# Single PSUM banks in turn for the expert passes, the passes' last part in common code, and a weight slot loaded from ScalarE's queue

## The chip, the cores and the metric

One Trainium2 chip, one core of it. The metric is the device time of one execution in microseconds (us); less is better. TensorE (PE) does the matrix products, VectorE (DVE) and ScalarE (ACT) read its results out of PSUM (eight banks of 2 KB per partition), GpSimd (POOL) issues the indexed transfers, SyncE (SP) most of the others.

## The reference

A banded attention, and behind it a layer of eight experts of which every token takes one. `x` has 3072 tokens of 512 numbers, an expert has 512 x 1024 and 1024 x 512 weights, all in float32:

```python
a = softmax(scale * q @ k.T + bias, over a band of 96 and the first 8 keys)
x = (a @ v) as (3072, 512)
expert_idx = argmax(x @ w_gate, axis=1)
probs = softmax(x @ w_gate)
gate_w = probs[n, expert_idx]
for e in range(8):
    mask = expert_idx == e
    h = maximum(x[mask] @ w1[e], 0)
    out[mask] = gate_w[mask] * (h @ w2[e])
```

## The kernel before

Attention takes the first 208 us of the span. Then comes the routing: tokens are scattered, sorted by expert, into a buffer in memory (`xs_dram`), and gathered from there. The experts run from about 246 us to 644 us, and a tail of 21 us ends the kernel.

**What an expert is made of.** The first 128 tokens of an expert e are its small part: `x_in_s(e)` (line 775) transposes them on PE into a PSUM tile and DVE copies them to `xsT` (line 776); `up_s(e)` (lines 786 and 790) multiplies by w1 and applies Relu on ACT; `down_s(e)` (lines 796 and 798) multiplies by w2, DVE multiplies by the gate into `ys`, and POOL scatters `ys` to the output. The rest of the tokens is its pass, n tokens wide. n is known only at run time, so the pass is written in 10 forms (n = 0, or 128 to 384 in steps of 32), and a switch at run time branches to one of them. With this input the passes e = 0 to 7 take the forms 352, 288, 256, 288, 256, 288, 288 and 160.

**What a form does**, in the order of PE's program, which is written by hand:
- up: for each of 8 slices f of the hidden layer, 4 matmuls into `ph` (line 893), then Relu on ACT into `hT` (line 895).
- `x_in(e+1, 0)` and `x_in(e+1, 1)` (line 858): 8 transposes of the next expert's tokens, which DVE copies to `xT` (line 859).
- down: for each of 4 slices d of the output, 8 matmuls into `py` (line 900), then an ACT copy into `yT` (line 902). From d = 1 on, `back(d-1)` stands behind each: it transposes `yT` on PE into a `pt` tile (line 881), and DVE multiplies by the gate into `y` (line 883 for the whole blocks of 128 tokens, line 887 for the rest).
- `x_in(e+1, 2)` behind `back(0)`, `x_in_s(e+2)` (line 775) behind `back(1)`; at the end of the form `back(3)` and then the scatters of `y` (line 733, on POOL; one for each begun block of 128 tokens).

**Common code between two forms**: the weights of expert e+3 are asked for on SP's queue, POOL gathers for e+2 and e+4, PE does `up_s(e+2)` and `down_s(e+2)`, and the next switch follows. PE, ACT, DVE and POOL all take part in the switch; SP doesn't.

**PSUM.** The two `ph` tiles have two banks each and hold two slices f each; there are two `pt` tiles and two `py` tiles of one bank, taken by the number of the block, the slice or the expert (d % 2, t % 2, e % 2). A wait goes by the tile, so a slice that is written into the second bank of a `ph` tile waits for the Relu that still reads the first one. The pools are the ones that the attention uses.

The weights lie in three slots. Those of experts 0 and 1 are loaded during the attention; the third slot lies where the attention's tiles were, and is loaded behind it by `fetch(2)`, four transfers of 1 MB on SP's queue. A float32 matmul of the program is two records in the trace.

```python
ph = self.ph[f // 2 % 2][:, f % 2, 0:n]      # up, slice f
pt, g = self.t[d % 2], self.gate[e % 2]      # back(d)
x, pt = self.xg[e % 2], self.t[t % 2]        # x_in(e, t)
x, pt = self.xs[e % 2], self.t[e % 2]        # x_in_s(e)
```

Of the kernel before, what the change touches and what calls it, by code (L numbers as in the profile page):

```python
# [20 lines left out]
def kernel(  # L21
# [666 lines left out]
    class Experts:  # L688
        def __init__(self, stack, rt, psum):
            self.rt = rt  # L690
            ps_s, ps_t, ps_o, ps_r = self.psum = psum
# [80 lines left out]
        def x_in_s(self, e):  # L772
            x, pt = self.xs[e % 2], self.t[e % 2]
# [8 lines left out]
        def up_s(self, e):  # L782
            for f in range(NFC):
                ph = self.ph[f // 4 % 2][:, 0, :]
                for c in range(NDC):
                    nc.tensor.matmul(ph[:, ts(f % 4, P)], lhsT=self.w[e % 3][0][:, c, ts(f, P)],  # L786
                                     rhs=self.xsT[e % 2][:, c, :], start=(c == 0), stop=(c == NDC - 1),
                                     skip_group_check=True)
                if f % 4 == 3:
                    nc.scalar.activation(self.hsT[:, f - 3:f + 1, :].rearrange("p a b -> p (a b)"), ph,  # L790
                                         AF.Relu)

        def down_s(self, e):
            py = self.py[e % 2]
            for f in range(NFC):
                nc.tensor.matmul(py[:], lhsT=self.hsT[:, f, :], rhs=self.w[e % 3][1][:, f, :],  # L796
                                 start=(f == 0), stop=(f == NFC - 1))
            nc.vector.tensor_scalar(self.ys[:], py[:], self.gates[:, e:e + 1], None, ALU.mult)  # L798
            self.scatter(self.ys[:], self.tos[:, e:e + 1])


        def begin(self, stack):

            ps_s, ps_t, ps_o, ps_r = self.psum
# [50 lines left out]
        def x_in(self, e, t):  # L855
            x, pt = self.xg[e % 2], self.t[t % 2]
# [10 lines left out]
        def one_pass(self, e, n, between):  # L867

            w1t, w2t = self.w[e % 3]
            xT, hT, y = self.xT[e % 2], self.hT, self.y[e % 2]  # L870
# [6 lines left out]
            def back(d):  # L877
                pt, g = self.t[d % 2], self.gate[e % 2]
                for t in range(0, n, P):
                    m = min(P, n - t)  # L880
                    nc.tensor.transpose(pt[0:m, t // P, :], self.yT[d % 2][:, t:t + m], ident[:])  # L881
                full = n // P
                nc.vector.tensor_tensor(y[:, 0:full, ts(d, P)], pt[:, 0:full, :],  # L883
                                        g[:, 0:full].unsqueeze(2).to_broadcast([P, full, P]), ALU.mult)
                if n % P:
                    m = n % P
                    nc.vector.tensor_scalar(y[0:m, full, ts(d, P)], pt[0:m, full, :], g[0:m, full:full + 1],  # L887
                                            None, ALU.mult)

            for f in range(NFC if n else 0):  # L890
                ph = self.ph[f // 2 % 2][:, f % 2, 0:n]
# [5 lines left out]
            for d in range(NDC if n else 0):  # L897
                py = self.py[d % 2][:, 0:n]
# [4 lines left out]
                if d:  # L903
                    back(d - 1)
                if d in (1, 2):
# [20 lines left out]
        def passes(self, judge):  # L926
            for e in range(E):
                index = {eng: self.forms[e] for eng in self.ENGINES}
                for i in tc.Switch(index, len(WIDTHS), hint=f"pass{e}"):
                    more = []  # L930
# [15 lines left out]
                if e + 3 < E:  # L946
                    self.up_s(e + 2)
                    self.down_s(e + 2)
                elif e + 2 < E:
                    self.up_s(e + 2)  # L950
                    judge()
                elif e + 1 < E:
                    self.down_s(e + 1)
# [4 lines left out]
    with ExitStack() as stack, tc.manual_schedule(engines={PE}):  # L958
        psum = [stack.enter_context(tc.tile_pool(name=f"ps_{nm}", bufs=n, space=bass.MemoryType.PSUM))
                for nm, n in (("s", 2), ("t", 2), ("o", 1), ("r", 1))]  # L960
        pool, rows = router_pools(stack)
        ex = Experts(stack, rt, psum)
        with ExitStack() as inner:
# [75 lines left out]
```

## Time and profile before

| | us |
|---|---|
| runs: median of 3 (lowest, highest) | 671.41 (669.81, 676.6) |
| the profiled execution | 667.69 |
| its span | 665.5 |
| PE busy in the span | 563.6 (85%) |
| DVE, ACT, POOL busy | 176.4, 125.2, 104.4 |
| mean granted clock of PE, of full speed | 0.965 |

The profile is of one execution. The span runs from the first to the last instruction that it shows; 2.2 us lie around it. The times in the rows below count from the start of the span.

### The profile page before, as it was taken

What the parts mean: (1) busy time and instruction counts of PE and PEld (TensorE: products, weight loads), DVE (VectorE), ACT (ScalarE), POOL (GpSimd) and SP (SyncE); (2) the same over time, 40 slices, a digit from 0 to 9 for tenths busy, and PEclk for the clock granted to TensorE, in tenths of its full rate; (3) what the DMA queues carried; (4) which work ended last, traced back from release to release, by engine and by line L of the source; (5) the groups of instructions that cost most, each with busy time, mean ns of one, the idle gap of its engine ahead of it and who ended that gap; (6) DMA issues with size and microseconds to landing.
All of it is one profiled execution on the core that took longest, in us unless ns stands there. A gap on an engine that the chain in (4) does not pass through costs nothing.

```text
span 665.5 us, 11159 instructions
## 1 busy us (share of the span) xinstructions
PE 563.6 (85%) x4541; PEld 434.8 (65%) x4541; DVE 176.4 (27%) x520; ACT 125.2 (19%) x237; POOL 104.4 (16%) x148
## 2 busy tenths in 40 slices
PE   3699699698799968999988898898999998889860
PEld 2588578587588635576666686577678576766660
DVE  6756456566363210110020020011001002002010
ACT  1353343435232001100100110110111110110100
POOL 3000400400501550013004002101301200100110
PEclk9799899999999989999998999999999999899995
DMA  9999997557513740334117035133433200100100
GB/s 165 250 258 215 271 233 169 166 138 159 178 33 118 258 146 0 126 91 135 57 75 226 1 127 179 51 127 105 127 126 131 68 0 3 58 0 3 40 24 19
DMA packets 98312, 77.48 MB, mean 116 GB/s; under 512 B 79194, under 2 KB 79194, under 8 KB 98144
## 3 DMA queue, kind: packets, MB, share of 16 engines
q1 hardware_dynamic: 90240, 56.63, 30.8%
q0 software_dynamic: 6544, 18.98, 8.8%
q8 instruction: 56, 0.92, 0.6%
q14 instruction: 112, 0.92, 0.4%
q10 hardware_dynamic: 1360, 0.04, 0.1%
HBM read 60.92 MB, written 12.89 MB: 111 GB/s over the span
## 4 chain that ended last, share of the span: by engine, by line
PE 70%; DVE 9%; issue 8%; ACT 4%; DMA 3%; POOL 2%; another core or an unknown queue 1%; ACTq 0%; POOLq 0%; DVEq 0%
PE ph L893 19%; PE py L900 18%; PE ph L786 8%; PE py L796 6%; PE po L358 4%; PE sp L336 4%; DVE p L347 2%; PE pr L369 2%; ACT hT L895 2%; PE pt L225 2%; PE px L380 2%; DMA xs_dram<-xr,slot_i 2%; PE pt L858 2%; PE pt L881 1%
## 5 line engine op out<-in xcount | busy, mean ns | idle before, releaser
L893 PE MATMUL ph<-xT,w 128*128 128x288 f32 (+3 forms) x512 | 131.1, 408 | 20.1 <-ACT hT L895 19.3
L893 PEld LDWEIGHTS ph<-xT,w 128*128 128x128 f32 x512 | 93.6, 194 | 58.5 <-ACT hT L895 33.0
L900 PE MATMUL py<-hT,w 128*128 128x288 f32 (+3 forms) x512 | 121.3, 393 | 0.0
L900 PEld LDWEIGHTS py<-hT,w 128*128 128x128 f32 x512 | 92.3, 190 | 21.3
L733 POOL DMA_INDIRECT out_dram<-y,to x21 | 20.5, 974 | 321.1 <-DVE y L887 241.4
L786 PE MATMUL ph<-xsT,w 128*128 128x128 f32 x512 | 61.2, 281 | 9.1 <-issue 3.7
L786 PEld LDWEIGHTS ph<-xsT,w 128*128 128x128 f32 x512 | 59.6, 196 | 11.6 <-issue 10.6
L348 ACT ACTIVATE p<-p 128x1024 f32<-128x1024 f32 (+1 forms) x48 | 47.0, 983 | 85.3 <-DVE p L347 78.2
L895 ACT ACTIVATE hT<-ph 128x288 f32<-128x288 f32 (+3 forms) x64 | 25.4, 397 | 180.7 <-PE ph L893 177.7
L796 PE MATMUL py<-w,hsT 128*128 128x512 f32 x128 | 56.3, 593 | 0.6 <-issue 0.6
L347 DVE SCALAR_TENSOR_TENSOR p<-sp,other 128x1024 f32<-128x1024 f32 x40 | 47.4, 1216 | 13.4 <-remote 11.6
L336 PE MATMUL sp<-qt,kt 64*128 64x128 f32 x448 | 41.0, 294 | 11.0 <-DVE p L347 7.2
L859 DVE COPY xT<-pt 128x512 f32<-128x512 f32 x24 | 15.8, 687 | 118.0 <-PE pt L858 118.0
L883 DVE TENSOR_TENSOR y<-pt,gate 128x256 f32<-128x256 f32 (+1 forms) x32 | 13.1, 408 | 119.5 <-PE pt L881 118.9
L358 PE MATMUL po<-p,vt 128*64 128x128 f32 x448 | 39.9, 277 | 4.7 <-issue 4.7
L336 PEld LDWEIGHTS sp<-qt,kt 64*128 64x128 f32 x448 | 34.0, 205 | 12.4 <-issue 11.7
L796 PEld LDWEIGHTS py<-w,hsT 128*128 128x128 f32 x128 | 23.7, 190 | 27.6 <-issue 27.6
L902 ACT COPY yT<-py 128x288 f32<-128x288 f32 (+3 forms) x32 | 12.3, 385 | 130.7 <-PE py L900 130.7
L358 PEld LDWEIGHTS po<-p,vt 128*64 128x64 f32 x448 | 27.3, 138 | 7.5 <-issue 7.3
L798 DVE TENSOR_SCALAR ys<-py,gates 128x512 f32<-128x512 f32 x8 | 6.0, 751 | 95.4 <-PE py L796 40.2
L336 PE MATMUL sp<-qt,ka 64*128 64x128 f32 x256 | 27.2, 290 | 0.0
L726 POOL DMA_INDIRECT xg<-xs_dram,grow x24 | 24.6, 1024 | 14.4 <-issue 6.1
(151 smaller groups left out, 498.2 us busy)
## 6 DMA issues: line engine op xcount, KB each, us to landing
w<-in_moe_w_dram SPq DMA_DIRECT2D x32, 1024.0 KB, 7.0
raw_q<-in_q_dram SPq DMA_DIRECT2D x24, 256.0 KB, 4.0
raw_k<-in_k_dram SPq DMA_DIRECT2D x24, 256.0 KB, 4.5
vt<-in_v_dram SPq DMA_DIRECT2D x24, 256.0 KB, 4.2
va<-vt SPq DMA_DIRECT2D x16, 192.0 KB, 4.1
va<-vt SPq DMA_DIRECT2D x16, 64.0 KB, 4.0
xs_dram<-xr,slot_i POOLq DMA_INDIRECT x24
xg<-xs_dram,grow POOLq DMA_INDIRECT x24
```

The lines of the kernel that those rows point to most:

```text
L336: nc.tensor.matmul(sp[:, a, j, t, :], lhsT=kt[r, 2 * g + j, :], rhs=qts[n][r, 2 * g + j, :], start=True, stop=True, skip_group_check=True)
L347: nc.vector.scalar_tensor_tensor(z, sc, QS, bi, ALU.mult, ALU.add)
L348: nc.scalar.activation(z, z, AF.Exp)
L358: nc.tensor.matmul(po[D * a:D * a + D, m, :], lhsT=vt[:, 2 * m + a, :], rhs=ps[n][m // 2][:, a, m % 2, t, :], start=(x == 0), stop=(x == l ...
L726: nc.gpsimd.indirect_dma_start(out=dst.bitcast(I32), out_offset=None, in_=xs_dram[:], in_offset=bass.IndirectOffsetOnAxis(ap=idx, axis=0), ...
L733: d = nc.gpsimd.indirect_dma_start(out=out[:], out_offset=bass.IndirectOffsetOnAxis(ap=idx, axis=0), in_=src, in_offset=None, bounds_check ...
L786: nc.tensor.matmul(ph[:, ts(f % 4, P)], lhsT=self.w[e % 3][0][:, c, ts(f, P)], rhs=self.xsT[e % 2][:, c, :], start=(c == 0), stop=(c == ND ...
L796: nc.tensor.matmul(py[:], lhsT=self.hsT[:, f, :], rhs=self.w[e % 3][1][:, f, :], start=(f == 0), stop=(f == NFC - 1))
L859: nc.vector.tensor_copy(out=self.xT[e % 2][:, :, ts(t, P)], in_=pt[:])
L893: nc.tensor.matmul(ph, lhsT=w1t[:, c, ts(f, P)], rhs=xT[:, c, 0:n], start=(c == 0), stop=(c == NDC - 1), skip_group_check=True)
L895: nc.scalar.activation(hT[:, f, 0:n], ph, AF.Relu)
L900: nc.tensor.matmul(py, lhsT=w2t[:, f, ts(d, P)], rhs=hT[:, f, 0:n], start=(f == 0), stop=(f == NFC - 1), skip_group_check=True)
```

## The change

Five things change in the experts, none in the attention:
- **PSUM.** The experts get a pool of their own, with eight tiles of one bank: three named `ph`, two `py`, three `t`. Each user takes the next one in turn. Slice f of the up part then uses the bank of slice f-3. The attention's pools are released before the experts begin.
- **Order in a form.** `x_in(e+1, 2)` moves behind `back(1)` and `x_in_s(e+2)` behind `back(2)`, which is the end of the form.
- **The last part.** `back(3)` and the scatters of `y` leave the form. `finish(e)` does them in common code, always for 384 tokens (3 transposes, 1 DVE multiply, 3 scatters), behind the first half of `up_s`, or in the last two passes behind the first half of `down_s(7)` and alone. Since unused rows are then read too, `clear_y` sets `y` and `yT` to zero once, on POOL. POOL takes no part in the switch any more.
- **Halves.** `up_s` and `down_s` are written in two halves; the work is the same.
- **Weights of expert 2.** `fetch(2)` is issued on ACT's queue, and stands behind `up_s(1)` in the program.

The core of the diff:

```diff
-        def fetch(self, e):
+        def fetch(self, e, queue=nc.sync):
...
-                    nc.sync.dma_start(out=dst[:, a:a + n // 2, :], in_=s_[:, a:a + n // 2, :])
+                    queue.dma_start(out=dst[:, a:a + n // 2, :], in_=s_[:, a:a + n // 2, :])
...
-            self.ph = [ps_s.tile([P, 2, 512], F32, tag="s", name=f"ph{i}") for i in range(2)]
-            self.t = [ps_t.tile([P, 4, P], F32, tag="t", name=f"pt{i}") for i in range(2)]
-            self.py = [ps_o.tile([P, 512], F32, tag="o", name="py0"),
-                       ps_r.tile([P, 512], F32, tag="r", name="py1")]
+            ps = stack.enter_context(tc.tile_pool(name="ps_e", bufs=1, space=bass.MemoryType.PSUM))
+            self.bank = {nm: [ps.tile([P, 4, P], F32, name=f"{nm}{i}") for i in range(n)]
+                         for nm, n in (("ph", 3), ("py", 2), ("t", 3))}
+        def turn(self, nm):
+            self.used[nm] += 1
+            return self.bank[nm][self.used[nm] % len(self.bank[nm])]
+        def clear_y(self):
+            for i in range(2):
+                nc.gpsimd.memset(self.y[i][:], 0.0)
+                nc.gpsimd.memset(self.yT[i][:], 0.0)
...
-                ph = self.ph[f // 2 % 2][:, f % 2, 0:n]
+                ph = self.turn("ph")[:].rearrange("p a b -> p (a b)")[:, 0:n]
...
                 if d:
-                    back(d - 1)
-                if d in (1, 2):
+                    self.back(e, d - 1, n)
                     other()
...
-            if n:
-                back(NDC - 1)
-            for t in range(0, n, P):
-                m = min(P, n - t)
-                self.scatter(y[0:m, t // P, :], self.to[e % 2][0:m, t // P:t // P + 1])
-        ENGINES = (PE, mybir.EngineType.Activation, mybir.EngineType.DVE, mybir.EngineType.Pool)
+        def finish(self, e):
+            self.back(e, NDC - 1, TP * P)
+            for t in range(TP):
+                self.scatter(self.y[e % 2][:, t, :], self.to[e % 2][:, t:t + 1])
+        ENGINES = (PE, mybir.EngineType.Activation, mybir.EngineType.DVE)
...
                         more.append(lambda: (self.x_in(e + 1, 0), self.x_in(e + 1, 1)))
+                        more.append(lambda: None)
                         more.append(lambda: self.x_in(e + 1, 2))
...
-                if e + 3 < E:
-                    self.up_s(e + 2)
-                    self.down_s(e + 2)
...
+                for fn in parts[:1] + [lambda: self.finish(e)] + parts[1:]:
+                    fn()
```

**PE, the form of 288 tokens of pass 3 and the common code behind it.** `ph`, `pt` (in the changed kernel `t`) and `py` with a number are PSUM tiles, `xs` the gathered tokens of a small part, `w_0` and `w_2` weight slots. Before:

```order
L893 MATMUL ph_2921<-xT_2911,w_0_131 128x288 x8
L893 MATMUL ph_2922<-xT_2911,w_0_131 128x288 x8
...
L881 MATMUL pt_2924<-ident,yT_2914 128x128 x2
L881 MATMUL pt_2924<-ident,yT_2914 32x128
L775 MATMUL pt_2924<-ident,xs_145 128x128 x4
L900 MATMUL py_2926<-hT,w_0_132 128x288 x8
L881 MATMUL pt_2923<-ident,yT_2913 128x128 x2
L881 MATMUL pt_2923<-ident,yT_2913 32x128
L881 MATMUL pt_2924<-ident,yT_2914 128x128 x2
L881 MATMUL pt_2924<-ident,yT_2914 32x128
...
L786 MATMUL ph_2921<-xsT_147,w_2_2906 128x128 x16
L786 MATMUL ph_2922<-xsT_147,w_2_2906 128x128 x16
```

And in the changed kernel:

```order
L891 MATMUL ph_2930<-xT_2915,w_0_119 128x288 x4
L891 MATMUL ph_2928<-xT_2915,w_0_119 128x288 x4
L891 MATMUL ph_2929<-xT_2915,w_0_119 128x288 x4
...
L869 MATMUL t_2935<-ident,xg_2912 128x128 x4
L898 MATMUL py_2932<-hT,w_0_120 128x288 x8
L912 MATMUL t_2933<-ident,yT_2917 128x128 x2
L912 MATMUL t_2933<-ident,yT_2917 32x128
L774 MATMUL t_2934<-ident,xs_133 128x128 x4
...
L786 MATMUL ph_2929<-xsT_135,w_2_2910 128x128 x16
L912 MATMUL t_2935<-ident,yT_2918 128x128 x3
L786 MATMUL ph_2930<-xsT_135,w_2_2910 128x128 x16
```

Eight matmuls in a row went to one `ph` tile, and now four do, with three tiles in turn. The transposes of `xs`, which had a whole down slice behind them, are now the last work of the form, directly ahead of the `up_s` that reads their copy; the form's last `back` stands between the halves of `up_s`.

**POOL, the end of the program.** `TENSOR_LOAD bad_i` reads the flag on which the kernel ends or runs again. Before:

```order
L733 DMA out_dram<-y_2916,to_2918 3072x512 x2
L929 ISA
L1034 UNCONDITIONAL_BRANCH
...
L733 DMA out_dram<-y_2916,to_2918 3072x512 x3
L1034 UNCONDITIONAL_BRANCH
L733 DMA out_dram<-ys,tos 3072x512
L1000 TENSOR_LOAD bad_i
```

And in the changed kernel:

```order
L732 DMA out_dram<-y_2919,to_2921 3072x512 x3
L732 DMA out_dram<-ys,tos 3072x512
L1061 UNCONDITIONAL_BRANCH
L732 DMA out_dram<-y_2920,to_2922 3072x512 x3
L1027 TENSOR_LOAD bad_i
```

The rows of before are two of the last pass's forms, of which the switch takes one, and the common code behind them, with the last scatter of `ys` in it. In the changed program POOL has no forms: one path, in which the last three scatters of `y` stand behind that of `ys`, directly ahead of the flag.

## Rows read from the trace of the kernel before

**Rows 1.** Page, engines: busy us (share of the span), records
```profile
PE 563.6 (85%) x4541; PEld 434.8 (65%) x4541; DVE 176.4 (27%) x520; ACT 125.2 (19%) x237; POOL 104.4 (16%) x148
```

**Rows 2.** PE's waits, 245 to 665 us: total us, times, longest
```profile
PE ph L893 <- ACT hT L895: 19.3, 32, 2.1
PE pt L858 <- DVE y L887: 3.8, 5, 0.8
PE ph L786 <- issue: 3.7, 2, 2.3
...
PE pt L775 <- DVE y L887: 2.3, 3, 0.8
```

**Rows 3.** Timeline, PE, pass 3: start, us, records, idle before
```profile
419.46 2.10 PE L893 MATMUL ph<-xT,w 128*128 128x288 f32 x8
...
426.90 4.15 PE L893 MATMUL ph<-xT,w 128*128 128x288 f32 x16 [0.56 <-ACT hT L895]
...
438.36 1.04 PE L858 MATMUL pt<-ident,xg 128*128 128x128 f32 x8
439.23 7.93 PE L900 MATMUL py<-hT,w 128*128 128x288 f32 x32
447.00 0.49 PE L881 MATMUL pt<-ident,yT 128*128 128x128 f32 x3
...
448.75 4.05 PE L900 MATMUL py<-hT,w 128*128 128x288 f32 x16
452.63 0.49 PE L881 MATMUL pt<-ident,yT 128*128 128x128 f32 x3
...
454.38 4.05 PE L900 MATMUL py<-hT,w 128*128 128x288 f32 x16
458.26 0.49 PE L881 MATMUL pt<-ident,yT 128*128 128x128 f32 x3
...
460.32 7.38 PE L786 MATMUL ph<-xsT,w 128*128 128x128 f32 x64 [0.81 <-DVE y L887]
...
474.41 1.89 PE L893 MATMUL ph<-xT,w 128*128 128x256 f32 x8
```

**Rows 4.** Timeline, PE, up slices of the passes of 256 and 160 tokens
```profile
379.17 3.72 PE L893 MATMUL ph<-xT,w 128*128 128x256 f32 x16 [0.53 <-ACT hT L895]
...
626.33 2.44 PE L893 MATMUL ph<-xT,w 128*128 128x160 f32 x16 [0.45 <-ACT hT L895]
```

**Rows 5.** Timeline, DVE, pass 3: behind `back(1)`
```profile
453.16 0.42 DVE L883 TENSOR_TENSOR y<-pt,gate 128x256 f32<-128x256 f32 x1 [3.52 <-PE pt L881]
453.50 0.33 DVE L887 TENSOR_SCALAR y<-pt,gate 32x128 f32<-32x128 f32 x1
...
454.58 0.69 DVE L776 COPY xsT<-pt 128x512 f32<-128x512 f32 x1 [0.75 <-PE pt L775]
```

**Rows 6.** Timeline, start of pass 6
```profile
576.12 0.41 ACT L895 ACTIVATE hT<-ph 128x288 f32<-128x288 f32 x1 [3.02 <-issue]
...
576.58 5.84 PE L893 MATMUL ph<-xT,w 128*128 128x288 f32 x16 [2.13 <-ACT hT L895]
```

**Rows 7.** Timeline, PE, `up_s` behind pass 1
```profile
355.00 6.47 PE L786 MATMUL ph<-xsT,w 128*128 128x128 f32 x41 [2.35 <-issue]
```

**Rows 8.** Windows: us, busy of PE, PEld, DVE, ACT, POOL, granted clock, DMA share
```profile
356.20:359.60 3.40, 3.40 (x19) 3.40 (x18) 0.00 (x0) 0.60 (x1) 1.56 (x2) 0.53 0.58 226
```

**Rows 9.** Timeline, the turn from attention to experts
```profile
207.27 0.60 PE L775 MATMUL pt<-ident,xs 128*128 128x128 f32 x4
208.73 0.68 DVE L401 TENSOR_TENSOR xr<-px,rden 128x512 f32<-128x512 f32 x1
218.11 1.05 POOL L205 DMA_INDIRECT xs_dram<-xr,slot_i  x1 [5.59 <-DVE inv_s L761]
```

**Rows 10.** Timeline, tail
```profile
644.09 0.98 POOL L733 DMA_INDIRECT out_dram<-y,to  x1 [25.74 <-DVE y L887]
...
650.32 0.98 POOL L733 DMA_INDIRECT out_dram<-ys,tos  x1 [4.07 <-issue]
```

More of the change, by code (lines that the diff above doesn't have):

```diff
@@ L772, in x_in_s @@
         def x_in_s(self, e):
-            x, pt = self.xs[e % 2], self.t[e % 2]
+            x, pt = self.xs[e % 2], self.turn("t")
             for c in range(NDC):
@@ L780, in x_in_s, with up_s, down_s @@
             nc.vector.tensor_copy(out=self.gates[:, e:e + 1], in_=x[:, DM:DM + 1])
-        def up_s(self, e):
-            for f in range(NFC):
-                ph = self.ph[f // 4 % 2][:, 0, :]
+        def up_s(self, e, half):
+            ph = self.turn("ph")
+            for i in range(NFC // 2):
+                f = half * (NFC // 2) + i
                 for c in range(NDC):
-                    nc.tensor.matmul(ph[:, ts(f % 4, P)], lhsT=self.w[e % 3][0][:, c, ts(f, P)],
+                    nc.tensor.matmul(ph[:, i, :], lhsT=self.w[e % 3][0][:, c, ts(f, P)],
                                      rhs=self.xsT[e % 2][:, c, :], start=(c == 0), stop=(c == NDC - 1),
                                      skip_group_check=True)
[L789 to L799, printed above, removed]
+            nc.scalar.activation(self.hsT[:, half * (NFC // 2):(half + 1) * (NFC // 2), :]
+                                 .rearrange("p a b -> p (a b)"), ph[:].rearrange("p a b -> p (a b)"), AF.Relu)
+        def down_s(self, e, half):
+            if half == 0:
+                self.pys = self.turn("py")
+            py = self.pys[:].rearrange("p a b -> p (a b)")
+            for f in range(half * (NFC // 2), (half + 1) * (NFC // 2)):
+                nc.tensor.matmul(py, lhsT=self.hsT[:, f, :], rhs=self.w[e % 3][1][:, f, :],
+                                 start=(f == 0), stop=(f == NFC - 1), skip_group_check=True)
+            if half:
+                nc.vector.tensor_scalar(self.ys[:], py, self.gates[:, e:e + 1], None, ALU.mult)
+                self.scatter(self.ys[:], self.tos[:, e:e + 1])
         def begin(self, stack):
-            ps_s, ps_t, ps_o, ps_r = self.psum
             pool = stack.enter_context(tc.tile_pool(name="pass", bufs=1))
@@ L855, in x_in @@
         def x_in(self, e, t):
-            x, pt = self.xg[e % 2], self.t[t % 2]
+            x, pt = self.xg[e % 2], self.turn("t")
             for c in range(NDC):
@@ L869, in one_pass @@
             w1t, w2t = self.w[e % 3]
[L870 removed]
+            xT, hT = self.xT[e % 2], self.hT
             between = list(between)
@@ L908, in one_pass, with back @@
                 other()
-            if n:
-                back(NDC - 1)
+        def back(self, e, d, n):
+            pt, g, y = self.turn("t"), self.gate[e % 2], self.y[e % 2]
             for t in range(0, n, P):
                 m = min(P, n - t)
-                self.scatter(y[0:m, t // P, :], self.to[e % 2][0:m, t // P:t // P + 1])
-        ENGINES = (PE, mybir.EngineType.Activation, mybir.EngineType.DVE, mybir.EngineType.Pool)
+                nc.tensor.transpose(pt[0:m, t // P, :], self.yT[d % 2][:, t:t + m], ident[:])
+            full, m = divmod(n, P)
+            if full:
+                nc.vector.tensor_tensor(y[:, 0:full, ts(d, P)], pt[:, 0:full, :],
+                                        g[:, 0:full].unsqueeze(2).to_broadcast([P, full, P]), ALU.mult)
+            if m:
+                nc.vector.tensor_scalar(y[0:m, full, ts(d, P)], pt[0:m, full, :], g[0:m, full:full + 1],
+                                        None, ALU.mult)
+        def finish(self, e):
[3 more added lines that the diff above has]
+        ENGINES = (PE, mybir.EngineType.Activation, mybir.EngineType.DVE)
         def load_forms(self):
@@ L945, in passes @@
                     self.hint(e + 1)
-                if e + 3 < E:
-                    self.up_s(e + 2)
-                    self.down_s(e + 2)
-                elif e + 2 < E:
-                    self.up_s(e + 2)
+                s_ = e + NS
+                if s_ + 1 < E:
+                    parts = [lambda: self.up_s(s_, 0), lambda: self.up_s(s_, 1),
+                             lambda: self.down_s(s_, 0), lambda: self.down_s(s_, 1)]
+                elif s_ < E:
+                    parts = [lambda: self.up_s(s_, 0), lambda: self.up_s(s_, 1)]
+                elif e + 1 < E:
+                    parts = [lambda: self.down_s(E - 1, 0), lambda: self.down_s(E - 1, 1)]
+                else:
+                    parts = []
+                for fn in parts[:1] + [lambda: self.finish(e)] + parts[1:]:
+                    fn()
+                if s_ == E:
                     judge()
-                elif e + 1 < E:
-                    self.down_s(e + 1)
     rt = Route("")
@@ L969 @@
         ex.x_in_s(0)
-        ex.up_s(0)
-        dispatch(pool, ex.t[0][:].rearrange("p t c -> p (t c)"), rt, xr, oh)
+        for half in range(2):
+            ex.up_s(0, half)
+        dispatch(pool, ex.turn("t")[:].rearrange("p t c -> p (t c)"), rt, xr, oh)
         ex.table()
@@ L977 @@
             ex.gather_s(e)
-        ex.fetch(2)
-        ex.down_s(0)
-        ex.up_s(1)
+        ex.clear_y()
+        for half in range(2):
+            ex.down_s(0, half)
+        for half in range(2):
+            ex.up_s(1, half)
+        ex.fetch(2, nc.scalar)
         ex.load_forms()
         ex.hint(0)
-        ex.down_s(1)
+        for half in range(2):
+            ex.down_s(1, half)
         ex.x_meta(0)
```

26 lines of the change are left out of this document (9 added, 17 removed).

## The prediction

> **What bounds the kernel now.** I read first the engines' busy time on the page: PE is busy for 563.6 of 665.5 us [rows 1], so nothing else can be the bound of the expert passes, and what can be won there is PE's idle time. Then PE's waits from 245 us on, where the passes run [rows 2]: the largest is the up part's wait for ACT's Relu, 19.3 us in 32 waits, that is four for each of the eight passes. Behind it come waits of some 0.8 us for DVE's multiply into `y`, by the transposes of line 858 (3.8 us in 5) and line 775 (2.3 us in 3), and 3.7 us in two gaps of `up_s` that nothing in the profile releases ("issue"). Then PE's timeline of one whole pass, number 3, 288 tokens wide [rows 3]: from its first record at 419.46 to the first of the next pass at 474.41 it takes 54.95 us, and each gap below can be seen in it.
>
> **The up part: single banks.** Slice f = 1 waits for the Relu of f = 0 only because both lie in one `ph` tile, and so at every odd slice. With three tiles in turn slice f waits for f-3, whose Relu (0.41 us) ended two slices earlier. In pass 3 the up part takes 438.36 - 419.46 = 18.90 us for 64 records. The down part, same width, same matmul, no wait, takes 447.00 - 439.23 = 7.77 us for 32, so 0.243 each [rows 3]; 64 such are 15.54 us. The gain is 3.36 us, 0.84 for each wait: 0.56 idle, and 0.27 which PE drains before it (16 records last 4.15, and 16 x 0.243 is 3.88). At 256 tokens the idle time is 0.53, at 160 tokens 0.45 [rows 4]; with the same 0.27 and four waits the gain is 3.2 and 2.9 us. For 352 tokens I take 3.3. Passes 1, 3, 5 give 3.36 each, passes 2 and 4 3.2 each, pass 0 3.3, pass 7 2.9: 22.7 us.
>
> Pass 6 has more to give. There ACT starts its first Relu 3.02 us late, with no releaser, PE waits 2.13 us for it, and then 16 records take 5.84 instead of 4.15 us [rows 6]. With three banks PE has three slices, 3 x 8 x 0.243 = 5.8 us, of work ahead of that wait and meets none. So besides 3.36 it wins 2.13 - 0.56 + 1.69 = 3.26: 6.6 us. **Sum of the up parts: 29.3 us.**
>
> **The three `t` banks.** In pass 3 `back(0)` with `x_in(4, 2)` occupies PE from 447.00 to 448.75, 1.75 us, and `back(1)` with `x_in_s(5)` from 452.63 to 454.38, 1.75 us; each has inside it the wait for DVE to have read the bank that was just written [rows 2, 3]. With three banks no writer meets the bank of the last two. Costs without a wait: three transposes of `back` 0.33 us (0.49 less the overlap with the next), four more 0.5 us. `back(0)` alone then costs 0.33, `back(1)` with `x_in` 0.83: 3.50 becomes 1.16, gain 2.3 us. This holds where DVE has two multiplies and `x_in_s` has the odd bank: passes 1, 3, 5. Even passes have less: `x_in_s` takes the other bank there, and at 256 tokens DVE has one multiply less. I take 1.4 in pass 0, 1.1 in passes 2 and 4, 0.9 in pass 6, which has no `x_in_s`, and nothing in pass 7: 6.9 + 1.4 + 2.2 + 0.9 = **11.4 us**.
>
> **The end of the form: a wait in place of another.** Now, in pass 3, `back(2)` starts at 458.26 and `up_s` at 460.32: 2.06 us, of it 0.81 waiting for DVE's last multiply [rows 3]. In the changed kernel `back(2)` and `x_in_s` end the form, and `up_s` waits for the copy `xsT`. DVE has that behind two multiplies: behind `back(1)` these ran from 453.16 to 453.83, 1.20 us after the 452.63 at which `back(1)` began; the copy takes 0.69 [rows 3, 5], and PE starts some 0.1 us after it: 1.99 us. `back(3)` in `finish` costs 0.33 more, always with three transposes, and no wait, since ACT's `yT` is long done. 2.32 for 2.06: a loss of 0.26 us; at 256 tokens by the same working 0.34. In passes 0 to 5 that loses 1.6 us; in pass 6, without `x_in_s`, the wait for `yT` goes and 0.6 us is won. **Net: a loss of 1.0 us.** What is queued behind the waiting matmul is PE's whole further program, so this wait counts in full. POOL's scatters now come about 4 us later and behind the gathers; the gathers come earlier, and nothing waits for `y` before its buffer is used again two passes later: nothing.
>
> **Start.** `x_in_s(0)` began at 207.27, beside DVE work that still read attention's banks. In the changed kernel it needs the released pools, so the end of DVE's last reader of them, line 401. That began at 208.73 and takes 0.68, with the copy `xsT` (0.69) ahead of it [rows 5, 9]; the copy will then be behind it. So it ends near 208.73 - 0.69 + 0.68 = 208.7, and `x_in_s(0)` begins near 208.8, 1.5 us later; `up_s(0)` and the routing behind it move as much. From that comes off about the length of one such copy, for which a transpose of `x_in(0)` waited for its bank. I take a loss of 1.0, between 0 and 2.8 (with 1.74 more, if PE comes out of the gap at half clock; the 1.74 is worked out below). `clear_y` runs on POOL in the 5.59 us for which POOL waits ahead of 218.11 [rows 9]. Its cost is not in the trace; at the rate of DVE's copy (512 numbers a partition in 0.69 us [rows 5]) the two `y` of 1536 and the two `yT` of 384 take 5.2 us, so they are just covered: nothing, or up to 0.5.
>
> **Weights of expert 2.** They are first read by `up_s(2)`, a whole pass behind the first (a pass is 55 us [rows 3]), and the experts' first matmuls stand ahead of that. Split between ACT's Relus they come some us later and take bandwidth from the scatters and gathers less at once: nothing, or 0.5 either way.
>
> **Tail.** The last two scatters of `y` go at 644.09 and 1.3 us later, then POOL has a gap of 4.07 with no releaser ahead of `ys` at 650.32 [rows 10]. In the changed kernel `ys` is ahead, and three scatters, 1.3 us apart, follow DVE's multiply: with PE's and DVE's branch 0 to 4 us late. Taken 1 to 2 us late, the last one is issued about 648.8: a gain of 1.5 us, between -1.5 and +2.6.
>
> **Sum.** 29.3 + 11.4 - 1.0 - 1.0 + 1.5 = 40.2 us. The span becomes 625.3, and with the 2.2 us around it the profiled execution 627.5. It lay 0.55% under the median of the runs (667.69 against 671.41); I put the median at 629.5.
>
> **What no row shows** is how much the program waits for its own code at the new branches. In the trace, `up_s` stood 2.35 us with no releaser in the middle of its records, and the 41 behind it took 6.47 us where they should take 41/64 of 7.38 = 4.73 [rows 3, 7], the granted clock being 0.53 of full, the 1.2 GHz level [rows 8], after PE had stood. That is 4.1 us for one such event; one more return has 1.3, the rest of the 3.7 in 2 [rows 2], the other five nothing. The change moves work out of the forms into code behind the branch, so the events may come and go: from nothing (a gain of about 5.4: 4.1 and 1.3) to all seven.
>
> The Trainium skill speaks against the change here ("Runtime: NRT & Kernel Launch", section "Instruction fetch mechanics"): code is fetched ahead only in sequence, and a taken branch whose target is not loaded stalls until it has been fetched. By that rule every return from a form could stall, as the first rival below has it; the trace agrees only in that gaps without a releaser stand behind some branches, not all.
>
> **Rivals.**
> - *Code stalls at each return.* If PE, in all seven returns with common PE work, stands as behind pass 1, 4.1 x 7 = 29 us come back, less the 5.4 that are there already: a span of 649, a run of 653. For it: the row of 2.35. Against it: five of seven returns show no such gap [rows 2]. Chance 0.10.
> - *The other side: PE waits for code at both ends of a form.* POOL's gap in the tail is 4.07 [rows 10], and ACT has one of 3.02 at the entry of a form [rows 6]. If code that moved behind the branch made PE stand 4.07 at each return and, what is loaded then having pushed out the next form, 3.02 at each entry, with 1.74 for the clock it would be 8.8 us a pass, 62 in seven, less the 5.4 that are there: 56 us back, a span of 682, a run of 686. It decides from (40.2 + 5.4) / 7 = 6.5 us a pass. Nothing of that size is on PE's rows; 2.35 is the largest [rows 7]. Chance 0.05.
> - *The change doesn't do what it says in the up part.* If PE still waited for ACT, because something else than the tile holds slice f, 29.3 us don't come: span 654.6, run 659. Against it: every other slice, which changes the tile, shows no wait: 32 waits for 64 slices [rows 2], 16 records between two of them [rows 3]. Chance 0.04.
>
> **How the numbers follow.** The sum has 0.81, with its own range: down to 616 (no code stalls 5.4, a start that costs nothing 1.0, the better tail 1.1, the 3.4 by which I raised the median over the profiled execution, and 0.3 a pass), up to 645 (three stalls more, 12.3, with the late start, 1.8, and part of the late tail). That holds just over 8 in 10, so it is the range given. About 1% is what a measurement of this kernel can tell from no change. Faster by over 1% (below 664.7) are the sum and the first and third rival: 0.95. The 0.05 of the other side is a band around its point of decision and above: 0.02 within 1%, 0.03 slower.
>
> **What would show it.** Right, if PE's up slices show no wait for ACT and 64 records at 288 tokens take 15.5 us; if line 774's transposes have no wait and `up_s` waits about 1.1 us for `xsT`; if a pass of 288 tokens takes about 49.5 us from start to start; if the first `x_in_s` starts near 208.8. The prediction is wrong where "issue" gaps on PE or ACT add up to over 10 us, where the granted clock falls in passes in which it was full, or where the first scatter into `xs_dram` starts over 3 us later than 218.11.

## The result, and the profile after

| | before | after |
|---|---|---|
| median of 4 runs (lowest, highest), us | 670.61 (668.74, 676.6) | 624.48 (622.65, 627.69) |
| the profiled execution, its span | 667.69, 665.5 | 626.1, 624.2 |
| PE busy in the span | 563.6 (85%) | 550.9 (88%) |

The ratio is 0.930, with a 95% interval of 0.923 to 0.938: 46 us less in the medians, 41.3 in the two profiled spans. The forecast was 629.5, in 616 to 645. (The 671.41 that it started from is the median of three of the four runs of before.)

The page of the changed kernel, busy us of each engine (share of the span), records:

```profile
PE 550.9 (88%) x4544; PEld 440.1 (71%) x4544; DVE 175.6 (28%) x514; ACT 125.7 (20%) x237; POOL 111.1 (18%) x155
```

PE's waits in the changed kernel from 243 us on (total us, times, longest), which answer [rows 2]:

```profile
PE ph L891 <- DVE xT L870: 6.8, 1, 6.8
PE ph L786 <- issue: 5.5, 6, 1.0
...
```

The 32 waits for the Relu are gone, and so are all waits for DVE's multiply. What is left is one wait of 6.8 us ahead of the first pass and six of 0.8 to 1.0 at the returns from the forms. The timeline of pass 3, PE (start, us, records, idle before), against [rows 3]:

```profile
405.72 15.68 PE L891 MATMUL ph<-xT,w 128*128 128x288 f32 x64
421.24 1.04 PE L869 MATMUL t<-ident,xg 128*128 128x128 f32 x8
...
429.87 0.49 PE L912 MATMUL t<-ident,yT 128*128 128x128 f32 x3
430.20 4.05 PE L898 MATMUL py<-hT,w 128*128 128x288 f32 x16
434.08 0.49 PE L912 MATMUL t<-ident,yT 128*128 128x128 f32 x3
434.41 0.60 PE L869 MATMUL t<-ident,xg 128*128 128x128 f32 x4
434.85 4.05 PE L898 MATMUL py<-hT,w 128*128 128x288 f32 x16
438.73 0.49 PE L912 MATMUL t<-ident,yT 128*128 128x128 f32 x3
439.06 0.60 PE L774 MATMUL t<-ident,xs 128*128 128x128 f32 x4
440.63 3.81 PE L786 MATMUL ph<-xsT,w 128*128 128x128 f32 x32 [0.97 <-issue]
444.27 0.49 PE L912 MATMUL t<-ident,yT 128*128 128x128 f32 x3
444.60 3.74 PE L786 MATMUL ph<-xsT,w 128*128 128x128 f32 x32
...
455.04 13.98 PE L891 MATMUL ph<-xT,w 128*128 128x256 f32 x64
```

The up part takes 421.24 - 405.72 = 15.52 us (18.90 before), `back(0)` 0.33, `back(1)` with `x_in` 0.77, and from `back(2)` to `up_s` it is 1.90. The pass takes 49.32 us from start to start, 5.63 less. The gains of all passes, start to start, in the same way: 3.69 (pass 0), 9.86, 5.84, 5.63, 4.30, 5.64, 8.84 (pass 6), and 2.86 in pass 7 up to its last `back`: 46.7 us. The turn from attention to experts (its rows, and those of the tail, come below) gives back 3.2 us of it, the tail wins 0.3, and the attention itself, which the change doesn't touch, ended 2.5 us later in this execution: 46.7 - 3.2 + 0.3 - 2.5 = 41.3.

### The profile page after: what moved, and what is told of

It reads as the page before. It is cut to its first block, busy times and chain, and to the rows that moved or that the text cites. A ratio compares the mean times of both kernels' runs of the same rounds, so it can differ in the third digit from the quotient of the medians.

```text
span 624.2 us, 11099 instructions
## 1 busy us (share of the span) xinstructions
PE 550.9 (88%) x4544; PEld 440.1 (71%) x4544; DVE 175.6 (28%) x514; ACT 125.7 (20%) x237; POOL 111.1 (18%) x155
## 5 line engine op out<-in xcount | busy, mean ns | idle before, releaser
L891 PE MATMUL ph<-xT,w 128*128 128x288 f32 (+3 forms) x512 | 121.8, 399 | 6.8 <-DVE xT L870 6.8
L891 PEld LDWEIGHTS ph<-xT,w 128*128 128x128 f32 x512 | 95.2, 193 | 34.0 <-DVE xT L870 7.0
L915 DVE TENSOR_TENSOR y<-t,gate 128x256 f32<-128x256 f32 (+2 forms) x32 | 14.3, 446 | 152.7 <-PE t L912 118.9
L732 POOL DMA_INDIRECT out_dram<-y,to x24 | 23.9, 996 | 123.8 <-DVE y L915 99.0
L870 DVE COPY xT<-t 128x512 f32<-128x512 f32 x24 | 15.6, 683 | 90.6 <-PE t L869 90.6
L225 PE MATMUL pt<-ident,raw_k 128*128 128x128 f32 x96 | 16.5, 299 | 13.8 <-issue 13.7
L358 PE MATMUL po<-p,va 128*64 128x128 f32 x256 | 27.4, 295 | 0.0
```

Source lines behind the costliest of these rows:

```text
L225: nc.tensor.transpose(pt[:, m, :], src[:, 2 * m:2 * m + 2, :].rearrange("p a d -> p (a d)"), ident[:])
L358: nc.tensor.matmul(po[D * a:D * a + D, m, :], lhsT=vt[:, 2 * m + a, :], rhs=ps[n][m // 2][:, a, m % 2, t, :], start=(x == 0), stop=(x == l ...
L732: d = nc.gpsimd.indirect_dma_start(out=out[:], out_offset=bass.IndirectOffsetOnAxis(ap=idx, axis=0), in_=src, in_offset=None, bounds_check ...
L891: nc.tensor.matmul(ph, lhsT=w1t[:, c, ts(f, P)], rhs=xT[:, c, 0:n], start=(c == 0), stop=(c == NDC - 1), skip_group_check=True)
```

## Experiments

**The banks of the up part alone.** In the kernel before, only `ph` is changed (with it the pool that it lies in, and the way `up_s` names the bank):

```diff
-            self.ph = [ps_s.tile([P, 2, 512], F32, tag="s", name=f"ph{i}") for i in range(2)]
+            self.ph = [ps.tile([P, 4, P], F32, name=f"ph{i}") for i in range(3)]
...
-                ph = self.ph[f // 2 % 2][:, f % 2, 0:n]
+                ph = self.ph[f % 3][:].rearrange("p a b -> p (a b)")[:, 0:n]
```

> The kernel before with one part of the change alone: the up part's `ph` is three single banks in turn instead of two tiles of two banks; order, `back`, `t`, `py`, the switch and the queues stay as before. Theory (the tile held the slice): PE's waits for the Relu in the up part (19.3 us in 32) go, 64 records at 288 tokens take 15.5 instead of 18.9 us, pass 6 also absorbs ACT's late start, and the run is 29 us shorter, about 641. The waits for the multiply into `y` stay (some 0.8 each), and so do PE's gaps without a releaser in `up_s` behind passes 1 and 2 (2.35 and 1.33 us), since the code behind the branches is laid out nearly as before. Rival (the 46 us came mostly from code that no longer has to be fetched, and little from the banks): 10 to 15 us shorter, about 657, or the gaps of 2.35 and 1.33 us go here too.

Measured: 643.28 us against 671.09 of the kernel before on the same chip, 0.960 (0.955 to 0.965): 27.8 us. PE's waits there, from 250 us on, and the gap behind pass 1 in its timeline:

```profile
PE pt L859 <- DVE y L888: 3.8, 5, 0.8
...
PE ph L786 <- issue: 2.3, 2, 2.2
PE pt L775 <- DVE y L888: 2.3, 3, 0.8
```
```profile
353.68 6.47 PE L786 MATMUL ph<-xsT,w 128*128 128x128 f32 x41 [2.16 <-issue]
```

No wait for the Relu is left; the waits for the multiply are the same 3.8 and 2.3 us as before [rows 2], and the gap behind pass 1 is still there, at the same record, with 41 records behind it [rows 7]. So the banks of the up part are worth what the theory says, and only that. (The gap behind pass 2 shrank from 1.33 to 0.18 us.)

**Two banks in place of three.** The changed kernel with fewer banks:

```diff
-                         for nm, n in (("ph", 3), ("py", 2), ("t", 3))}
+                         for nm, n in (("ph", 2), ("py", 2), ("t", 2))}
```

> The changed kernel with two `ph` banks and two `t` banks instead of three each, still taken in turn (six PSUM banks used). Theory A (splitting and taking banks in turn is what counts): a slice lasts 1.08 to 2.4 us and its Relu 0.3 to 0.45, so slice f finds the Relu of f-2 done; and in the turn the writer of a `t` bank comes one down slice after its last reader. No wait returns, the time is that of the changed kernel, 624 within 1. Theory B (the third banks carry it, as the prediction put it for `t`): the waits of some 0.8 us behind `back` return in passes 0 to 6, about 11 us, 635; and if the third `ph` bank is needed, pass 6 shows ACT's late start as a wait of 1 us or more.

Measured: 627.40 us, 0.935 (0.931 to 0.940), against 0.930 (0.923 to 0.938) of the changed kernel: the intervals overlap. Its timeline, PE, pass 3:

```profile
406.34 15.68 PE L891 MATMUL ph<-xT,w 128*128 128x288 f32 x64
...
441.25 3.81 PE L786 MATMUL ph<-xsT,w 128*128 128x128 f32 x32 [0.97 <-issue]
```

No wait returns, in pass 6 neither, and every pass from 1 to 6 takes the changed kernel's time within 0.02 us. So theory A: the third banks are worth nothing that these rows show. For `ph` what counts is that a bank is a tile of its own, as the experiment above shows. The `t` tiles had one bank each before; there two things changed together, and no run has one without the other: the next writer takes the bank that has been at rest for longest, where before it took the one given by its number, and `x_in(e+1, 2)` and `x_in_s` moved in the form. By the numbers of before, the new order alone would still have put `x_in_s` on the bank that `back(2)` had just filled in the even passes, and no other writer directly on the bank just written; so how much of the gain is the turn stays open.

**`back(3)` and the scatters back in the form.**

```diff
             while between:
                 other()
+            if n:
+                self.back(e, NDC - 1, n)
+            for t in range(0, n, P):
+                m = min(P, n - t)
+                self.scatter(self.y[e % 2][0:m, t // P, :], self.to[e % 2][0:m, t // P:t // P + 1])
...
-        ENGINES = (PE, mybir.EngineType.Activation, mybir.EngineType.DVE)
+        ENGINES = (PE, mybir.EngineType.Activation, mybir.EngineType.DVE, mybir.EngineType.Pool)
...
-                for fn in parts[:1] + [lambda: self.finish(e)] + parts[1:]:
+                for fn in parts:
```

> The changed kernel with one part undone: `back(3)` at the pass's own width and the scatters of `y` stand in the form again, behind `x_in_s`, and POOL takes part in the switch again. Theory A (the move only orders work; PE's gaps of before went with the layout of the code, not with the move): `up_s` then waits for a further DVE multiply, some 0.4 us a pass, 3 us in all; 627 to 628, with POOL's gap of about 4 us at the end of the program back. Theory B (the move out of the form took away the code stalls): gaps of 1.3 to 2.4 us without a releaser return on PE behind some passes, with half clock behind them, 5.4 us more: 632 to 634.

Measured: 634.24 us, 0.944 (0.939 to 0.948); on the same chip the kernel with two banks each, whose passes are those of the changed kernel, had 627.40. PE's timeline behind pass 1:

```profile
346.69 0.49 PE L917 MATMUL t<-ident,yT 128*128 128x128 f32 x3
348.42 1.46 PE L786 MATMUL ph<-xsT,w 128*128 128x128 f32 x11 [1.23 <-DVE y L923]
352.99 8.57 PE L786 MATMUL ph<-xsT,w 128*128 128x128 f32 x53 [3.10 <-issue]
```

The further multiply costs less than was expected where it stands alone: pass 3 takes 49.58 instead of 49.32 us (pass 6, which has no `x_in_s` ahead of its last `back`, takes 1.3 us more, 0.2 of it a wait for ACT's `yT` and 0.6 one without a releaser). But the gaps without a releaser are back, 3.10 us behind pass 1 and 1.50 behind pass 2; these two passes take 55.34 and 47.11 instead of 49.32 and 45.45. Theory B: the move out of the form is what took the gaps away. Three things moved at once here; the next two kernels separate them.

**The same, without POOL in the switch; and POOL alone in the switch.** The one has `back(3)` in the form but the scatters in common code; the other is the changed kernel with POOL among the switch's engines:

```diff
             while between:
                 other()
+            if n:
+                self.back(e, NDC - 1, n)
...
-            self.back(e, NDC - 1, TP * P)
```
```diff
-        ENGINES = (PE, mybir.EngineType.Activation, mybir.EngineType.DVE)
+        ENGINES = (PE, mybir.EngineType.Activation, mybir.EngineType.DVE, mybir.EngineType.Pool)
```

> As in_form on PE, ACT and DVE (`back(3)` at the pass's own width inside the form), but the scatters of `y` stand in common code behind the small part's work and POOL takes no part in the switch. Theory A (PE's gaps behind passes 1 and 2 come when POOL, sent to another place in its code at the same moment, has to load code too): the gaps of 3.1 and 1.5 us of in_form and the half clock behind them are gone, and the time falls from 634 to about 626, some 2 us above the changed kernel for the further multiply that `up_s` waits for. Theory B (they come from how PE's own code lies with `back(3)` in the form): PE's code is the same as in in_form, so the gaps stay, 633 to 634.

> The changed kernel with one word more: POOL takes part in the switch again, with nothing to do in any form; PE's, ACT's and DVE's programs are those of the changed kernel. Theory A (POOL's jumps and the code it loads delay PE's code): gaps without a releaser of 1 us or more return on PE behind some passes, 5 us or more in all, 630 or above. Theory B (the layout of PE's own code): PE's rows are those of the changed kernel, 624 within 1.5; POOL may pay a few us at the end of the program.

Measured: 633.55 us (0.950; 0.942 to 0.958) for the first, 621.83 (0.931; 0.923 to 0.938) for the second, on the same chip. Behind pass 1 PE's timeline has, without POOL:

```profile
341.68 0.49 PE L914 MATMUL t<-ident,yT 128*128 128x128 f32 x3
343.40 0.91 PE L786 MATMUL ph<-xsT,w 128*128 128x128 f32 x6 [1.23 <-DVE y L920]
348.49 4.68 PE L786 MATMUL ph<-xsT,w 128*128 128x128 f32 x26 [4.19 <-issue]
```

and with POOL alone:

```profile
343.43 3.81 PE L786 MATMUL ph<-xsT,w 128*128 128x128 f32 x32 [0.97 <-issue]
```

So theory B in both: with `back(3)` in the form the gaps stand, 4.19 us behind pass 1 and 3.16 behind pass 2, without POOL; with POOL in the switch and `back(3)` outside they don't. POOL's part of the move is worth nothing that was measured; PE's part carries it. What PE waits for in the gap is seen in the queues that carry instructions. The DMA queues of a stretch (packets, MB, share of 16 engines), first the kernel without POOL, from 336 us, in the last but one down slice, to the first record of `up_s` at 343.4:

```profile
q0 software_dynamic: 39, 0.16, 12.3%
q1 hardware_dynamic: 28, 0.06, 3.1%
q14 instruction: 1, 0.01, 1.1%
```

and from there to 348.6 us, the end of the gap:

```profile
q1 hardware_dynamic: 695, 1.39, 79.8%
q0 software_dynamic: 190, 0.33, 19.0%
q8 instruction: 1, 0.02, 1.1%
...
```

then the changed kernel at the same return, from 342 us to the first record of `up_s` at 345.86, and from there to 351:

```profile
...
q1 hardware_dynamic: 101, 0.21, 22.9%
q8 instruction: 1, 0.02, 1.4%
```
```profile
q1 hardware_dynamic: 793, 1.59, 85.9%
q0 software_dynamic: 156, 0.23, 12.6%
q14 instruction: 3, 0.02, 1.1%
```

The block of 16 KB on q8 comes 2.6 us behind the start of `up_s` in the kernel with the gap, and 3.1 us ahead of it in the changed one. At the returns from passes 0 to 4 it is the same: 2.1 to 4.7 us behind the start in the four kernels with `back(3)` in the form, the kernel before among them, and 2.0 to 4.1 ahead of it in the six others (2.9 to 4.0 in the changed one). (At the return from pass 5 it comes 0.7 us ahead to 0.2 behind in the four, and no gap stands there.) The gaps end with the block: in the four kernels with gaps, two returns each, all eight gaps end 1.3 to 1.6 us behind the end of that packet. They stand 6 to 47 records into `up_s`, and in each kernel 20 or 24 records later behind pass 2 than behind pass 1; going on like that, PE would come to the place behind passes 3 and 4 only when the block was in, which would be why these two have no gap (an estimate from these places; it leaves pass 0 open).

In the gap the DMA engines are full (from 344.5 to 348.4 us their mean busy share is 1.02), mostly with weights on q1; but they are as full in the changed kernel behind its block (the shares above add up to 1.00), and the packet itself took 0.93 us in the gap and 0.88 in the changed kernel. So that the weights make the block late is not seen; how long it waited ahead of its packet no view shows.

Shown is that the block is late where `back(3)` ends the form, and that PE's gaps end with it. That q8 carries PE's code is inferred, from the 16 KB and from these times. Why the request is late is only argued: the form's last instruction, which waits for ACT's last `yT`, keeps PE's own queue from getting past the branch while PE still works on the last down slice. (In passes 0 to 5 of the two kernels that put `back(3)` back into the form no time is lost to that wait itself.) The rival is that the code lies differently with `back(3)` in the form. A kernel that puts a wait at the end of a form without moving any code would tell; it was not run.

**The last wait at the return.** The changed kernel with `back(2)` moved into common code too, and `x_in_s` one down slice earlier:

```diff
-                if d:
+                if 0 < d < NDC - 1:
                     self.back(e, d - 1, n)
                     other()
...
-            self.back(e, NDC - 1, TP * P)
+            for d in (NDC - 2, NDC - 1):
+                self.back(e, d, TP * P)
...
-                        more.append(lambda: None)
```

> The changed kernel with `back(2)` moved into common code too, beside `back(3)`, and `x_in_s` one down slice earlier, so that DVE's copy `xsT` is done when the form ends. Theory A (PE's gap of 0.83 to 0.98 us at each return, put down to issue, is the wait for `xsT`): the gap goes in all six returns, 5.5 us less, about 619. Theory B (it is the branch, or code that has to be fetched): it stays at some 0.8 to 1.0 us, and the time is that of the changed kernel, 624.

Measured: 617.11 us, 0.920 (0.916 to 0.924), the fastest of all here, 10.3 us below the kernel with two banks on the same chip. Its return from pass 1, and the only wait of PE from 245 us on:

```profile
338.86 4.05 PE L898 MATMUL py<-hT,w 128*128 128x288 f32 x16
342.74 2.51 PE L786 MATMUL ph<-xsT,w 128*128 128x128 f32 x21
```
```profile
PE ph L891 <- DVE xT L870: 6.0, 1, 6.0
```

Theory A: `up_s` follows the last slice without a gap in all six returns, and a pass of 288 tokens takes 48.12 us, 1.20 less. The 0.97 that the profile puts down to "issue" was the wait for `xsT`; its releaser isn't seen behind the branch. (In the changed kernel's pass 3 the copy `xsT` ends at 440.53, and `up_s` starts at 440.63.) The gain is larger than the 5.5 expected: of the 9.7 us between the two profiled spans the returns give 6.8, pass 0's up part 1.1 and the tail 1.9, where the last scatter is issued 2.1 us earlier; the last two were not forecast. Behind the first pass's wait of 6.0 us the profile shows no wait of PE in the passes of this kernel.

**The start: four pools in place of one.** The experts' eight banks lie in four pools that match the attention's, with the banks first used in the scores' place:

```diff
+            for k, part in enumerate((("t1", "t2", "ph1", "ph2"), ("t0", "ph0"), ("py0",), ("py1",))):
+                ps = stack.enter_context(tc.tile_pool(name=f"ps_e{k}", bufs=1, space=bass.MemoryType.PSUM))
```

> The changed kernel with its eight PSUM banks in four pools that lie where the attention's four lay, so that the bank of the first `x_in_s` depends on the scores' readers alone and not on DVE's last read (line 401). Theory A (the late start is that wait): `x_in_s(0)` begins 0.16 us behind the attention's last transpose instead of 1.88, the first scatter into `xs_dram` 11.0 us behind it instead of 12.8 or 14.4, and the run is 1.7 us shorter (up to 3.4 where PE came out of the wait at half clock): 621 to 623. Theory B (the late start is the weights on ACT's queue or `clear_y` on POOL): the first scatter stays at 12.8 or more.

First what there is to win, in the changed kernel. Its timeline at the turn (PE's last transpose of the attention, the first of the experts, `up_s(0)`, and the first scatter), against [rows 9]:

```profile
209.59 0.33 PE L381 MATMUL pr<-ident,rs 128*128 128x128 f32 x1
211.47 0.63 PE L774 MATMUL t<-ident,xs 128*128 128x128 f32 x4 [1.55 <-issue]
212.92 9.04 PE L786 MATMUL ph<-xsT,w 128*128 128x128 f32 x64 [0.82 <-DVE xsT L775]
```
```profile
224.00 1.05 POOL L205 DMA_INDIRECT xs_dram<-xr,slot_i  x1 [6.17 <-DVE inv_s L760]
```

`x_in_s(0)` stands 1.88 us behind the attention's last transpose (0.16 in the kernel before), and `up_s(0)` takes 9.04 us where the same 64 records behind the passes take 7.55. The granted clock was 0.81 there. With the same 1.88 us it takes 7.41 at the full clock in three other profiles, and 8.75 to 8.77 at 0.84 in three more; so the late start doesn't always cost this. In the four pools' timeline:

```profile
206.02 0.33 PE L381 MATMUL pr<-ident,rs 128*128 128x128 f32 x1
206.18 0.60 PE L774 MATMUL t<-ident,xs 128*128 128x128 f32 x4
...
243.22 0.75 DVE L800 TENSOR_SCALAR ys<-py,gates 128x512 f32<-128x512 f32 x1 [6.94 <-DMA out_dram<-ys,tos]
```

The wait is gone, and the first scatter comes 11.0 us behind the attention's last transpose instead of 14.4: theory A on the place. But the time, 621.07 us, is 0.931 (0.924 to 0.938), no less than the changed kernel's, and 621.83 is that of the POOL kernel beside it. The rows say where it went: the first pass starts 39.8 us behind the attention's last transpose, where it was 42.1 in the changed kernel's profile; but in the five other kernels with its late start and its queue it was 39.7 to 42.0. So no gain at the first pass stands out from what this stretch varies by. From the first scatter to the first pass it is 28.8 us here, the longest of all: DVE stands 6.94 us for the transfer of the other expert's `ys` ahead of the copies that the pass needs.

**The weights back on SP's queue.**

```diff
-        ex.fetch(2, nc.scalar)
+        ex.fetch(2)
```

> The changed kernel with `fetch(2)` back on SP's queue, all four transfers at once. Theory A (the queue is worth nothing, the weights are read 80 us later): the first scatter and the first pass start as in the changed kernel, 624 within 1.5. Theory B (four transfers of 1 MB at once delay the scatters and gathers that lead to the first pass): the stretch from the first scatter to the first pass, 27.7 us, gets longer by 1 us or more. Theory C (the transfers on ACT's queue hold up the Relus of the start): it gets shorter.

Measured: 622.44 us, 0.932 (0.924 to 0.938), the changed kernel's ratio. From the first scatter to the first pass it is 26.4 us, where the changed kernel had 27.7 and the six other kernels with ACT's queue 26.6 to 28.8. That is the shortest, by 0.1 us and in one execution of each, and the time doesn't show it: theory A, as far as these numbers go.

## Why the prediction was right

**The up part** was the largest term and came as worked out: 15.52 us for 64 records at 288 tokens (15.54 forecast), no wait, and pass 6 with ACT's late start absorbed (6.65 us from first to last up record, 6.6 forecast). All up parts together won 28.6 us for 29.3; the difference is pass 0, which won 2.4 instead of 3.3. The granted clock in it was 0.86 (0.92 before); PE had stood 6.79 us ahead of it, where before it had stood 5.56 and 0.78 with four transposes between. The kernel with the `ph` banks alone shows the gain by itself (3.6 us in its pass 0).

**The `t` banks:** the size was right (`back(0)` 0.33, `back(1)` with `x_in` 0.77, forecast 0.33 and 0.83; 12.0 us in all passes for 11.4), the reason only in part. The prediction said that with three banks no writer meets the last two. That is so, but with two in turn none meets the last one either, and no wait is left. The step should have gone through the turn bank by bank: a down slice of some 4 us, or half of `up_s`, lies between a bank's writer and its next one. What the new order does by itself the prediction didn't ask, and no run shows it.

**The end of the form:** 1.90 us from `back(2)` to `up_s` for 1.99, and 0.33 for `back(3)`. Right in pass 3, and the wait that took the other's place is as long as forecast; the kernel with `back(2)` in common code shows that it is this wait. Over all passes the end of the form won 0.2 us where a loss of 1.0 was forecast: passes 0 to 5 lost 0.9 for 1.6, pass 6 won 1.15 for 0.6.

**Code that has to be fetched** was the step that was mis-sized. The prediction left the two gaps of before as they were (5.4 us) and had a rival in which all seven returns get one. They went instead: pass 1 won 9.86 us where pass 3 of the same width won 5.63, and pass 2 5.84 where pass 4 won 4.30; the difference is 5.8 us. The step asked what lies behind the branch, and not what PE does ahead of it; that `back(3)` at the end of the form brings the gaps is shown, by what way it does is argued. By the Trainium skill ("Runtime: NRT & Kernel Launch", section "Instruction fetch mechanics") a taken branch to code that isn't loaded stalls until it has been fetched, and code is loaded in blocks of 16 KiB. The trace agrees on the blocks (16 KB each on q8) and has gaps of 0.2 to 4.2 us that end with one; they stand 6 to 47 records behind the branch, behind two passes only, and at the same returns a block that came 2.0 us or more ahead of `up_s` cost nothing. The rival that every return stalls didn't come true, nor did the one of stalls at both ends of a form.

**The start** lost 3.2 us, beyond the 2.8 of its bound, for 1.0 taken. `x_in_s(0)` came 1.7 us later as worked out (1.5). But `up_s(0)` ran 1.6 us longer in this execution, which the bound had, and the 0.7 of a copy that was to come off did not. In the five other kernels with this start the loss was 0.8 to 3.0 us, against the one profile of before. Here the prediction's own sign of being wrong was met: the first scatter, at 224.00, starts 5.9 us later than 218.11, where over 3 was the sign; 2.5 of them are the attention's later end, 3.4 the start's own. `x_in(0)` indeed no longer waits for a bank, but the first pass waits for DVE all the same:

```profile
249.12 0.75 DVE L800 TENSOR_SCALAR ys<-py,gates 128x512 f32<-128x512 f32 x1 [7.80 <-DMA out_dram<-ys,tos]
249.78 1.88 DVE L870 COPY xT<-t 128x512 f32<-128x512 f32 x3
...
251.71 22.17 PE L891 MATMUL ph<-xT,w 128*128 128x352 f32 x64 [6.79 <-DVE xT L870]
```

These are rows of the changed kernel. There is one `ys` tile; expert 1's result waits until that of expert 0 is scattered, which POOL does behind eight gathers, and the copies `xT` of the first pass stand behind it in DVE's order. So the first pass hangs on POOL's line of transfers, by these rows. The 22.17 us for records that take 18.9 at the down part's rate (9.47 for 32) are its late clock: 0.86 of full was granted there. A second `ys` tile was not run.

**The tail** won 0.3 us for 1.5. The end of the changed kernel:

```profile
602.03 0.55 PE L912 MATMUL t<-ident,yT 128*128 128x128 f32 x3 [0.22 <-ACT yT L900]
...
604.97 0.56 DVE L915 TENSOR_TENSOR y<-t,gate 128x384 f32<-128x384 f32 x1 [2.59 <-issue]
605.81 0.98 POOL L732 DMA_INDIRECT out_dram<-y,to  x1 [19.89 <-DVEq L1029]
...
608.37 0.98 POOL L732 DMA_INDIRECT out_dram<-y,to  x1 [0.30 <-issue]
```

POOL's gap of 4.07 [rows 10] is gone, but DVE has one of 2.59 behind its branch, where 1 to 2 us were taken, and it and three scatters stand in line. Counted from the last pass's `back(2)` the last scatter is issued 0.9 us earlier than before, for 1.5 forecast; the rest of the miss lies behind it, up to the end of the span (15.1 us before, 15.9 now). What takes longer there wasn't looked for.

**The sum.** The span was forecast at 625.3 and is 624.2: the code gaps took 5.8 off and the other passes 1.2 (the measured 46.7, less 5.8, for 39.7), the start gave 2.2 back, the tail 1.2 and the attention 2.5. Terms that were missed on both sides nearly cancel: that the span came within 1.1 us is luck, though the terms of the passes, without the code gaps, came within 1.2 us of their 39.7. The median lies 5 us below the forecast: the profiled execution took 1.4 less than the 627.5 forecast for it, and the median lies 1.6 below it instead of 2.0 above. (The range's lower end takes off 3.4 us for that step up to the median; the forecast had put on 2.0.)

## What to carry to other kernels

Where a wait goes by the tile, two results in one tile cost a drain and a refill of the pipe at every second one; make each bank a tile and take banks in turn, and then check by the order whether two are not enough. Give an engine that branches work ahead of the branch that waits for nothing, and look at when the code behind the branch arrives: in these kernels a last `back` was better placed behind the branch, between pieces of work that is ready, and the block on q8 then came in time (why it did is argued, not shown). And when a gain at one place is bounded by a queue behind it, look at what else stands in the order of the engine that releases it: here, by the rows, one `ys` tile holds the whole first pass. The gains that were found on the way (the return without a wait, the earlier first scatter, two `ys` tiles) were not run in one kernel.

## What the runs showed of the hardware

- A block of 16 KB on the instruction queue q8 (by inference PE's code) came 2.0 to 4.1 us ahead of the first work behind a branch in six kernels, and 2.1 to 4.7 us behind it in the four whose form ends in the transposes of ACT's last result. With the late ones PE stood 0.2 to 4.2 us behind two of the passes, and each such gap ended 1.3 to 1.6 us behind the end of the block's packet, which itself took 0.9 to 1.1 us.
- With POOL in the switch, and nothing else changed, q14 has 114 packets instead of 83; the time is the same (0.931 and 0.930 of the kernel before).
- Behind the same wait of 1.88 us at the start PE had the full clock in three profiles (64 records of `up_s(0)` in 7.41 us) and 0.81 to 0.84 of it in four (8.75 to 9.04 us).
- The attention, the same in all kernels, had its last transpose between 206.0 and 213.1 us in ten profiles, and by up to 3.6 us apart on one chip; passes 1 to 6 repeat to 0.02 us in the five kernels that have them in the changed kernel's order. What moves the attention was not looked for, and it is larger than several of the terms above; the kernel before has one profile.
